# Pooled attention with routed experts: longer warm-up, own PSUM banks for the first pooled v, constants on either side of the first pooled k, and search steps moved in front of the last attention tiles

## The chip, the cores and the metric

The kernel runs on one core of one Trainium2 chip. The time is the device time of one execution in microseconds (us), and less is better. Before the change three runs took 638.83, 641.46 and 642.39 us, so the median is 641.46 us. A profile comes from one execution more, whose own device time was 640.09 us.

## What is computed

Attention over keys and values that are averaged in groups of 8 rows, followed by a layer of 8 experts with a greedy assignment of tokens. The sizes are B = 8, H = 8, S = 576, D = 64, N = 4608 tokens of width 512, E = 8 experts of hidden width 1024, and cap = N / E = 576 tokens for each expert.

```python
# k_p, v_p: mean over 8 rows in sequence (72 rows left)
attn = softmax(q @ k_p.T / 8); x = (attn @ v_p) as (N, 512)
logits = x @ w_gate                      # (N, 8)
# greedy: pairs (token, expert) by falling logit; a pair is taken when the token
# is still free and the expert holds fewer than cap tokens
for e in range(8):
    out[tokens of e] = relu(x[tokens of e] @ w1[e]) @ w2[e]
```

## The kernel before

The program has two parts. There is no scheduler: each engine runs its instructions in the order in which the Python code issues them, so the place of a call in the code is its place in the queue of every engine that it uses.

**Attention** (class `Attention`) works on 36 tiles of 128 rows. A batch has four and a half tiles, so tile 4 is the first that also holds rows of batch 1. For each tile TensorE makes the scores of all heads (`st_s`, L205, into the PSUM tile `pss`, which has one buffer), VectorE takes the maximum and subtracts it (`softmax`, L215 and L216), ScalarE takes the exponential (L217), TensorE transposes the result in two groups (`st_e`, L234, into `pse` and `rt`), ScalarE copies it out (`eT`, L235), TensorE multiplies it with the pooled v (`st_av`, L247, into `psa`, two buffers), and VectorE normalizes (`norm`: L259, L262 and L272, with the gate logits `lg` in L265 once for four tiles). The loop in `run` is a pipeline: turn n issues the scores of tile n, the transposes of tile n-1, the product of tile n-2 and the normalization of tile n-3.

Keys and values are pooled by `pool_k` (L146 to L150, into `kblk`) and `pool_v` (L161 to L163 into `vsum`, then the masked copies L167 or L176 into the blocks `vblk`). Batch 0 is pooled by VectorE ahead of tile 0 and in turn 0, in two pieces each since k and v arrive in two pieces; the other batches are pooled by GpSimd while the loop runs. `prep_v` (L186, L188) transposes `vsum`, and `prep_g` (L195, L196) multiplies it with the gate weights `wblk` and puts the result into eight columns of `vblk`. Both take the single PSUM bank `rt`, which the second group of `st_e` also takes. The constants of the routing are made in `Routing.consts`. `warm(n)` issues n products of a matrix of ones, whose result is never used.

**Routing** (class `Routing`) finds the tokens of one expert after the other by a search with four rounds (`search`): VectorE compares the rank of each token with 32 thresholds (`compare`, L563, into `cmp`), TensorE counts (L568 for the first expert), and the range shrinks (L630 and L635). `best` (L511, L514, L517) makes each token's best expert (`oh`) and its place on the scale (`q16`) from the logits. For the first expert both run in part ahead of the end of attention: `after` is a table from a tile number to functions that are called behind this tile's `norm`, and `begin` is called in pieces by `finish`, which handles the last two tiles. `close` turns the result into the expert's number (`eid`, which starts the load of its weights) and its list of rows (L699), which starts the five gathers on GpSimd (L929); then it counts what is taken (`per` L708, `pc` L711, L714, and the small VectorE operations L716 to L736).

**Experts** (function `experts`): the generator `g` of the routing is advanced by `step` at places that estimated times in the code set (`now`, `ready`, `dve`). Before the first expert the code waits for its rows, calls `step(0)` (L1182), splits the first four pieces of the weights (L937 and L941), asks for the other half of them through a copy named `late`, calls `step(0)` again (L1187), issues 8 warm-up products and transposes the first two groups of tokens (`turn`, L961 into `tp`, L963, L965). Then stage 1 (L985) and stage 2 (L1012, L1023) of each expert follow.

Of the kernel before, what the change touches and what calls it, by code (L numbers as in the profile page):

```python
# [9 lines left out]
F32 = mybir.dt.float32  # L10
# [11 lines left out]
class Attention:  # L22
# [44 lines left out]
    def local(self, loc, full, consts, then):  # L67
# [84 lines left out]
    def pool_v(self, b, eng, c=slice(0, 5), first=False):  # L152
# [17 lines left out]
        for m0, m1 in ((0, 1), (1, 2), (2, 5)):  # L170
            m0 = max(m0, c.start)
            if m0 < m1:
                n = m1 - m0
                o = slice(B[m0], B[m1])
                k = (B[m1] - B[m0]) // n
                eng.tensor_tensor(v[:, o, :64].rearrange("p (c i) d -> p c i d", c=n),  # L176
                                  s[:, m0:m1, None, :].to_broadcast([128, n, k, 64]),
                                  self.mask[:, o, None].rearrange("p (c i) d -> p c i d", c=n)
                                  .to_broadcast([128, n, k, 64]), op=OP.mult)
# [10 lines left out]
    def prep_g(self, b):  # L190

        nc = self.nc
        ps = self.psR.tile([128, 512], F32, name="rt")
# [109 lines left out]
    def run(self, ctx, full, consts, after, end, warm):  # L303
# [27 lines left out]
        self.local(ctx.enter_context(tc.tile_pool(name="loc", bufs=1)), full, consts,  # L331
                   lambda: self.pool_k(0, nc.vector, kh))
# [10 lines left out]
        for n in range(nt):  # L343
# [16 lines left out]
            if n == 0:  # L360
                self.pool_v(0, nc.vector, vh[1])
# [16 lines left out]
class Routing:  # L378
# [20 lines left out]
    def consts(self, jp, ident):  # L399
# [13 lines left out]
        nc.vector.tensor_scalar(self.wts, self.i36[:, :8], -1.0, 8.0, op0=OP.mult, op1=OP.add)  # L413
        self.tri = cst.tile([128, 128], BF, name="tri")
# [3 lines left out]
        self.jp = jp  # L418
# [10 lines left out]
        self.upper = cst.tile([128, 1], F32, name="upper")  # L429
        nc.vector.tensor_scalar(self.upper, self.pcol, 64.0, None, op0=OP.is_ge)  # L430
        self.need = cst.tile([128, 8], F32, name="need")
        nc.vector.memset(self.need, float(self.cap))
        self.code = cst.tile([128, NC], F32, name="code")
        nc.vector.memset(self.code, 0.0)
        self.bad = cst.tile([128, 1], F32, name="bad")
        nc.vector.memset(self.bad, 0.0)
        self.gs = [cst.tile([128, 16], BF, name=f"g{i}") for i in range(2)]
        self.shares = cst.tile([128, self.rounds], F32, name="shares")
        for i in range(self.rounds):
            nc.vector.memset(self.shares[:, i:i + 1], (J * SHRINK) ** -i / J)  # L440
# [110 lines left out]
    def search(self, shadow, spare):  # L551
# [18 lines left out]
        for k in range(rounds):  # L570
# [4 lines left out]
            elif k == 0:  # L575

                compare(0, nb - 1)
                yield 0
# [165 lines left out]
    def begin(self, g):  # L744

        next(g)
        self.best(self.NC - 4, self.NC - 2)
# [15 lines left out]
    def phase(self, k):  # L763
# [18 lines left out]
        if k == 0:  # L782
            self.nc.gpsimd.tensor_copy(self.lg0, self.lg)
# [248 lines left out]

@with_exitstack
def kernel(ctx, tc, q, k, v, wblk, moe_w1, moe_w2, out):
# [15 lines left out]
    with ExitStack() as c2:  # L1050
# [3 lines left out]
        A.run(c2, R.ones, lambda: R.consts(A.jp, A.ident), {NC - 11: [step], NC - 10: [step], NC - 9: [step], NC - 5: [lambda: R.best(0, NC - 4)]},  # L1054
# [8 lines left out]
def experts(ctx, tc, g, R, xd, w1, w2, out, ident, cap):  # L1063
# [118 lines left out]
    step(0)  # L1182
# [4 lines left out]
    step(0)  # L1187
# [6 lines left out]
    now, ready, dve = 0.0, 0.0, 2.0  # L1194
# [128 lines left out]
```

## Time and profile before

| | us | where it stands |
|---|---|---|
| device time, median of 3 runs | 641.46 | 638.83 to 642.39 |
| profiled execution, device time | 640.09 | 1.37 below the median |
| its span, first to last instruction | 638.2 | 1.89 less than its device time |
| first scores of tile 0 | 7.66 | rows of TensorE, L205 |
| scores of tile 35, the last | 136.39 | same |
| rows of the first expert known | 161.31 | end of L699 |
| stage 1 of the first expert starts | 168.61 | TensorE, L985 |
| one expert in the middle | 57.4 | 289.4 to 346.8 |
| busy: TensorE, VectorE, ScalarE, GpSimd | 603.2, 396.9, 244.1, 174.0 | first part of the page |

In the rows of the profile PE is TensorE's products, PEld its loads of weights, DVE VectorE, ACT ScalarE, POOL GpSimd and SP the queue that issues most loads. A row of the timeline gives the start, the duration, the engine, the line, the operation, output and input tile with the shape, the number of operations that were merged, and in brackets the idle time before it with what ended that. A row of the table by stretches gives, for each stretch, the busy time of PE, PEld, DVE, ACT and POOL with the number of operations, then the clock granted to TensorE (1.00 is full), the busy share of the transfer engines and GB/s.

### The profile page before, as it was taken

How to read it: one execution, taken by the hardware profiler on the slowest of the kernel's cores; microseconds unless marked ns; L12 is line 12 of the kernel's file. 1: busy time of each engine (PE TensorE's matmuls, PEld its weight loads, DVE VectorE, ACT ScalarE, POOL GpSimd, SP SyncE). 2: the span in 40 equal slices, each digit the busy share in tenths (PEclk: the TensorE clock that was granted, in tenths of full speed). 3: DMA queues.
4: the chain of work that ended last, by engine and by line, in shares of the span. 5: the costliest groups of instructions: out<-in, count | busy, mean ns of one | idle time of the engine just before them, and what ended most of it. 6: DMA issues, size and time to landing. Idle time of an engine off the chain costs nothing.

```text
span 638.2 us, 11819 instructions
## 1 busy us (share of the span) xinstructions
PE 603.2 (95%) x4516; PEld 522.3 (82%) x4516; DVE 396.9 (62%) x1142; ACT 244.1 (38%) x561; POOL 174.0 (27%) x215
## 2 busy tenths in 40 slices
PE   6999999994799999999999999999999999999991
PEld 3899998984598789779977987897799889879980
DVE  7677777888886768766862885386378236506100
ACT  6344444442362335233532433252345225415210
POOL 1999996000300410312111302120230213020011
PEclk9799999997799999999999999999999999999996
DMA  9989982121630743308103701630190054013010
GB/s 359 426 333 385 348 311 84 67 83 51 207 134 1 256 157 123 101 34 298 67 17 113 284 1 49 225 139 18 50 339 8 37 207 170 17 64 128 1 51 29
DMA packets 32578, 92.13 MB, mean 144 GB/s; under 512 B 3456, under 2 KB 3456, under 8 KB 29824
## 3 DMA queue, kind: packets, MB, share of 16 engines
q1 hardware_dynamic: 21296, 62.92, 26.5%
q0 software_dynamic: 5888, 18.88, 8.4%
q10 hardware_dynamic: 5328, 9.48, 3.9%
q8 instruction: 37, 0.61, 0.4%
q14 instruction: 29, 0.24, 0.1%
HBM read 72.40 MB, written 18.87 MB: 143 GB/s over the span
## 4 chain that ended last, share of the span: by engine, by line
PE 72%; issue 14%; DVE 7%; POOL 3%; DMA 2%; ACT 1%; POOLq 0%; SPq 0%; ACTq 0%; DVEq 0%
PE h L985 25%; PE h L1012 20%; PE psa L247 7%; PE pss L205 6%; PE h L1023 3%; PE tp L961 2%; PE pse L234 2%; POOL out_dram L999 1%; PE rt L234 1%; PE rt L195 1%; POOL xg L929 1%; PE rt L688 1%; PE rt L605 1%; PE rt L186 1%; PE rt L568 1%
## 5 line engine op out<-in xcount | busy, mean ns | idle before, releaser
L999 POOL DMA_INDIRECT out_dram<-yt,rows x32 | 33.2, 1036 | 280.5 <-ACT yt L1016 280.1
L1012 PE MATMUL h<-w2l,hh 128*128 128x512 f32 x256 | 102.8, 401 | 0.0
L1012 PE MATMUL h<-w2h,hl 128*128 128x512 f32 x256 | 102.0, 399 | 0.0
L1012 PE MATMUL h<-w2h,hh 128*128 128x512 f32 x256 | 101.2, 395 | 0.0
L985 PE MATMUL h<-xl,w1h 128*128 128x320 f32 (+1 forms) x512 | 95.9, 302 | 0.0
L985 PE MATMUL h<-xh,w1h 128*128 128x320 f32 (+1 forms) x512 | 91.2, 299 | 0.7 <-ACT xh L963 0.7
L985 PE MATMUL h<-xh,w1l 128*128 128x320 f32 (+1 forms) x512 | 91.7, 298 | 0.0
L990 ACT ACTIVATE hh<-h 128x320 fp32r<-128x320 f32 (+1 forms) x128 | 51.9, 409 | 99.1 <-PE h L985 96.9
L985 PEld LDWEIGHTS h<-xh,w1h 128*128 128x128 f32 x512 | 75.3, 189 | 3.6 <-issue 2.7
L985 PEld LDWEIGHTS h<-xl,w1h 128*128 128x128 f32 x512 | 77.0, 190 | 0.7
L985 PEld LDWEIGHTS h<-xh,w1l 128*128 128x128 f32 x512 | 76.1, 189 | 0.2
L965 DVE TENSOR_TENSOR xl<-tp,xh 128x512 fp32r<-128x512 f32 (+1 forms) x40 | 25.3, 633 | 78.7 <-ACT xh L963 78.4
L993 DVE SCALAR_TENSOR_TENSOR hl<-h,hh 128x320 fp32r<-128x320 f32 (+1 forms) x128 | 57.4, 451 | 25.3 <-ACT hr L992 16.3
L929 POOL DMA_INDIRECT xg<-xd,rows x40 | 39.7, 992 | 96.6 <-DVE rows L699 62.9
L1016 ACT ACTIVATE yt<-h 128x512 f32<-128x512 f32 x32 | 19.1, 597 | 119.7 <-PE h L1012 103.8
L247 PE MATMUL psa<-vblk,eT 128*128 128x146 f32 (+3 forms) x400 | 61.9, 303 | 0.0
L1012 PEld LDWEIGHTS h<-w2h,hl 128*128 128x128 f32 x256 | 48.1, 188 | 9.0
L1012 PEld LDWEIGHTS h<-w2l,hh 128*128 128x128 f32 x256 | 48.4, 189 | 8.2
L1012 PEld LDWEIGHTS h<-w2h,hh 128*128 128x128 f32 x256 | 48.2, 188 | 8.3
L247 PEld LDWEIGHTS psa<-vblk,eT 128*128 128x128 f32 (+1 forms) x400 | 52.2, 181 | 1.7 <-DVE xt L272 0.3
L205 PE MATMUL pss<-kblk,rawq 128*128 128x144 f32 (+1 forms) x320 | 45.9, 302 | 3.6 <-DVE e L216 2.8
L941 DVE TENSOR_TENSOR w1l<-raw,w1h 128x512 fp32r<-128x512 f32 x64 | 41.2, 686 | 8.1 <-ACT w1h L937 7.9
(194 smaller groups left out, 905.4 us busy)
## 6 DMA issues: line engine op xcount, KB each, us to landing
raw<-in_moe_w_dram SPq DMA_DIRECT2D x64, 512.0 KB, 6.8
xd<-xt ACTq DMA_DIRECT2D x36, 256.0 KB, 4.3
rawv<-in_v_dram SPq DMA_DIRECT2D x7, 1280.0 KB, 11.5
rawk<-in_k_dram SPq DMA_DIRECT2D x7, 1152.0 KB, 8.1
rawq<-in_q_dram SPq DMA_DIRECT2D x7, 1152.0 KB, 13.5
rawk<-in_k_dram SPq DMA_DIRECT2D x2, 576.0 KB, 4.6
rawv<-in_v_dram SPq DMA_DIRECT2D x1, 768.0 KB, 7.2
rawq<-in_q_dram SPq DMA_DIRECT2D x1, 640.0 KB, 8.7
```

The source lines that it names most:

```text
L205: nc.tensor.matmul(ps[cols, j // 2, 144 * (j % 2):144 * (j % 2) + 144], self.q_of(b, j, n, cols.stop - cols.start), self.kblk[b % 4][:, j] ...
L234: nc.tensor.transpose(ps[:127, 128 * m:128 * m + 128], self.e[i][:, o:o + 127], self.ident)
L247: self.nc.tensor.matmul(o[h], self.eT[i][:, c, h], self.vblk[b % 4][:, self.BLOCKS[c]:self.BLOCKS[c + 1]], start=(c == cs[0]), stop=(c == ...
L929: nc.gpsimd.indirect_dma_start(out=self.xg[:n, t, :], out_offset=None, in_=self.xd, in_offset=bass.IndirectOffsetOnAxis(ap=rows[:n, t:t + ...
L941: self.nc.vector.tensor_tensor(l, raw, h.bitcast(F32), op=OP.subtract)
L965: later(1.3, 0.65, lambda: nc.vector.tensor_tensor(xl, ps[:, :, :n], xh, op=OP.subtract))
L985: nc.tensor.matmul(ps[:, :m], a[:, j, fs], b[:, j, o], start=(n == 0), stop=(n == 11))
L990: nc.scalar.activation(hh[:, f, o], ps[:, :m], AF.Relu)
L993: later(0.65, 0.4, lambda f=f, o=o, m=m, ps=ps: nc.vector.scalar_tensor_tensor(hl[:, f, o], ps[:, :m], 0.0, hh[:, f, o].bitcast(F32), op0= ...
L999: st = nc.gpsimd.indirect_dma_start(out=rows, out_offset=bass.IndirectOffsetOnAxis(ap=idx, axis=0), in_=y, in_offset=None)
L1012: nc.tensor.matmul(ps, a[:, f, o], b[:, f], start=(f == 0 and k == 0), stop=(f == 7 and k == 2))
L1023: nc.tensor.matmul(ps[64 * a:64 * a + 64, :256], self.hr[:, f], self.raw2[e][:, f, 256 * a:256 * a + 256], start=(f == 0), stop=(f == 7))
```

## The change

1. `consts` is split. The first half (numbers 0 to 35, `colv`, `j16`, `pcol`, `wts`, `upper`, `need`, `code`, `bad`, `shares`) now stands ahead of `pool_k(0)`, the rest (`more`: `tri`, `untri`, `spread`, `blk`, `gs`) behind it; before, all of it stood behind.
2. Turn 0 issues 16 warm-up products where it issued 8.
3. `prep_v(0)` and `prep_g(0)` take the two banks of a `psa` buffer in place of `rt`, and `prep_v(0)` stands ahead of the transposes of tile 0. The masked copy of the second piece of the first pooled v (`vblk`, L176) goes from VectorE to GpSimd.
4. For batch 1 `prep_v` is one turn later, and `prep_g` stands inside turn `first[1] + 2` = 6, ahead of the product that needs it.
5. `best` for tiles 0 to 27 is called behind tile 28 (before: tiles 0 to 31 behind tile 31); the large comparison of the first search round is cut into three pieces, of which two stand behind tiles 29 and 30 and the third in `begin`.
6. A new function `wake` gathers 32 rows of the second weights by an indirect transfer on GpSimd, behind tile 30 in the code; its result is not used. The copy of the logits `lg0` goes from GpSimd to ScalarE.
7. Before the first expert the two calls of `step(0)` are taken out, and one stands behind the first two `turn`s, with other estimated times.

```diff
@@ local
-        then()
-        consts()
+        consts()
+        then()
+        more()
@@ pool_v
-                eng.tensor_tensor(v[:, o, :64]...
+                (blocks or eng).tensor_tensor(v[:, o, :64]...
@@ prep_v
-        ps = self.psR.tile([128, 512], F32, name="rt")
+        if b:
+            ps = self.psR.tile([128, 512], F32, name="rt")
+        else:
+            self.ps0 = self.ps.tile([128, 2, 512], F32, name="psa", bufs=2)
+            ps = self.ps0[:, 0]
@@ prep_g
-        ps = self.psR.tile([128, 512], F32, name="rt")
+        ps = self.psR.tile([128, 512], F32, name="rt") if b else self.ps0[:, 1]
@@ run
-            plan(first[b], self.prep_v, b)
-            plan(first[b] + 1, self.prep_g, b)
+            plan(first[b] + (b == 1), self.prep_v, b)
+            if b > 1:
+                plan(first[b] + 1, self.prep_g, b)
...
             if n == 0:
-                warm(8)
+                warm(16)
+            if n == 1:
+                self.prep_v(0)
             if n >= 1:
                 self.st_e(n - 1, 0)
+            if n == first[1] + 2:
+                self.prep_g(1)
...
-            if n == 1:
-                self.prep_v(0)
...
-                self.pool_v(0, nc.vector, vh[1])
+                self.pool_v(0, nc.vector, vh[1], blocks=nc.gpsimd)
@@ search
-                compare(0, nb - 1)
-                yield 0
+                for b0, b1 in ((0, 4), (4, 7), (7, nb - 1)):
+                    compare(b0, b1)
+                    yield 0
@@ begin
+        self.best(self.NC - 8, self.NC - 2)
         next(g)
-        self.best(self.NC - 4, self.NC - 2)
@@ phase
-            self.nc.gpsimd.tensor_copy(self.lg0, self.lg)
+            self.nc.scalar.activation(self.lg0, self.lg, AF.Copy)
@@ new
+def wake(nc, R, wk, w2):
+    row = wk.tile([32, 512], F32, name="norow", bufs=1)
+    nc.gpsimd.indirect_dma_start(out=row, out_offset=None, in_=w2.rearrange("e f d -> (e f) d"),
+                                 in_offset=bass.IndirectOffsetOnAxis(ap=R.ti[:32, 0:1], axis=0))
@@ the table behind tiles
-NC - 5: [lambda: R.best(0, NC - 4)]
+NC - 8: [lambda: R.best(0, NC - 8)], NC - 7: [start], NC - 6: [start, lambda: wake(nc, R, rwk, moe_w2)]
@@ experts
-    step(0)
     w1 = pieces[0] = Pieces(0, X.high1, X.low1)
     for i in range(4):
         w1.next(i < 3)
     X.load_1(behind(0), 2, 4)
-    step(0)
     warm(8)
...
-    now, ready, dve = 0.0, 0.0, 2.0
+    step(0)
+    now, ready, dve = 0.0, 2.6, 2.6
```

Three places show what this does to the queues. The first is TensorE in turns 1 and 2: the scores of tile 1 (`pss`), the transposes of the exponentials `e` and of the pooled sums `vsum`, the gate products (`wblk`), and the scores of tile 2. Before:

```order
L205 MATMUL pss<-kblk_128,rawq 128x144 x4
L234 MATMUL pse<-ident,e 127x128 x3
L234 MATMUL rt<-ident,e 127x128 x2
L186 MATMUL rt<-ident,vsum 128x128 x3
L195 MATMUL rt<-wblk,vT 128x40
L195 MATMUL rt<-wblk,vT 128x32
L195 MATMUL rt<-wblk,vT 128x16
L205 MATMUL pss<-kblk_128,rawq 128x144 x4
```

The same stretch of TensorE after the change (line numbers have moved with the code):

```order
L211 MATMUL pss<-kblk_128,rawq 128x144 x4
L192 MATMUL psa<-ident,vsum 128x128 x3
L240 MATMUL pse<-ident,e 127x128 x3
L240 MATMUL rt<-ident,e 127x128 x2
L201 MATMUL psa<-wblk,vT 128x40
L201 MATMUL psa<-wblk,vT 128x32
L201 MATMUL psa<-wblk,vT 128x16
L211 MATMUL pss<-kblk_128,rawq 128x144 x4
```

The transposes of the pooled sums have moved ahead of those of the exponentials, and they and the gate products write to `psa`, so they no longer share a bank with `rt`.

The second is VectorE around the last two tiles: the normalization of tile 31, then the best experts (`bv`, `q16a`, `oh`) and the softmax of tile 35 (`mx`, `e`). Before:

```order
L265 TENSOR_REDUCE lg<-gt_1505 128x32
L272 TENSOR_TENSOR xt<-psa,rinv 128x512
L511 TENSOR_REDUCE bv_241<-lg 128x32
L514 TENSOR_SCALAR q16a<-bv_241,lo_239,scale 128x32
L517 TENSOR_TENSOR oh_243<-lg,bv_241 128x256
L215 TENSOR_REDUCE mx<-pss 128x8
L216 TENSOR_TENSOR e<-pss,mx 128x576
```

After, from the same normalization on, to the third piece of the comparison:

```order
L271 TENSOR_REDUCE lg<-gt_1512 128x32
L278 TENSOR_TENSOR xt<-psa,rinv 128x512
L221 TENSOR_REDUCE mx<-pss 128x8
L222 TENSOR_TENSOR e<-pss,mx 128x576
L265 RECIPROCAL rinv<-psa 128x8
L268 TENSOR_TENSOR gt_1662<-psa,rinv 128x64
L271 TENSOR_REDUCE lg<-gt_1662 128x8
L278 TENSOR_TENSOR xt<-psa,rinv 128x512
```

The three operations of `best` no longer stand between the normalization of tile 31 and the softmax of tile 35; for tiles 0 to 27 they stand four tiles earlier, and tiles 28 to 33 come behind tile 33.

The third is VectorE between the list of rows and stage 1 of the first expert. Before, the counting of what is taken (`per`, `pc`, `left` and on) stands on both sides of the split of the weights (`w1l`) and ahead of the tokens' low parts (`xl`):

```order
L699 CAST rows<-rt 128x5
L703 SCALAR_TENSOR_TENSOR halves<-rt,upper 128x1
L708 TENSOR_TENSOR per<-oh_243,sel 128x288
L711 TENSOR_REDUCE pc<-per 128x8
L941 TENSOR_TENSOR w1l<-raw_1974,w1h 128x512 x4
L1179 COPY late<-eid 1x1
L716 TENSOR_TENSOR left<-need,rt 128x8
```

After the change:

```order
L713 CAST rows<-rt 128x5
L717 SCALAR_TENSOR_TENSOR halves<-rt,upper 128x1
L955 TENSOR_TENSOR w1l<-raw_1985,w1h 128x512 x4
L1202 COPY late<-eid 1x1
L979 TENSOR_TENSOR xl<-tp,xh 128x4x128 x2
L722 TENSOR_TENSOR per<-oh_243,sel 128x288
L725 TENSOR_REDUCE pc<-per 128x8
L1007 SCALAR_TENSOR_TENSOR hl<-h,hh 128x256
L730 TENSOR_TENSOR left<-need,rt 128x8
```

The counting now stands behind the low parts of the first two groups of tokens, inside stage 1 (`hl` is an output of stage 1). On TensorE the product of `pc` (L714) moves with it, from ahead of the 8 warm-up products to behind the third group of tokens.

More of the change, by code (lines that the diff above doesn't have):

```diff
@@ L65, in consts, with local @@
         self.jp = jp
-    def local(self, loc, full, consts, then):
+    def local(self, loc, full, consts, more, then):
         nc = self.nc
@@ L150, in pool_k, with pool_v @@
                 eng.tensor_tensor(self.kblk[b % 4][h, c, y], t2[h, c, 0], t2[h, c, 1], op=OP.add)
-    def pool_v(self, b, eng, c=slice(0, 5), first=False):
+    def pool_v(self, b, eng, c=slice(0, 5), first=False, blocks=None):
         src = self.rv[b]
@@ L301, in finish, with run @@
             self.store(t, xt)
-    def run(self, ctx, full, consts, after, end, warm):
+    def run(self, ctx, full, consts, more, after, end, warm):
         tc, nc = self.tc, self.nc
@@ L417, in consts @@
         nc.vector.tensor_scalar(self.untri, self.tri, -31.0, None, op0=OP.mult)
-        self.jp = jp
         t = cst.tile([128, 32], I32, name="tf")
@@ L1053 @@
         step = lambda: next(bounds, None)
-        A.run(c2, R.ones, lambda: R.consts(A.jp, A.ident), {NC - 11: [step], NC - 10: [step], NC - 9: [step], NC - 5: [lambda: R.best(0, NC - 4)]},
+        start = lambda: next(g)
+        A.run(c2, R.ones, lambda: R.consts(A.jp, A.ident), R.more, {NC - 11: [step], NC - 10: [step], NC - 9: [step], NC - 8: [lambda: R.best(0, NC - 8)],
+                                                       NC - 7: [start], NC - 6: [start, lambda: wake(nc, R, rwk, moe_w2)]},
               R.begin(g), R.warm)
```

29 lines of the change are left out of this document (16 added, 13 removed).

## Prediction

> **What bounds the kernel now.** The page first: the share of TensorE and the line of its granted clock in 40 slices of 16 us.
>
> ```profile
> PE 603.2 (95%) x4516; PEld 522.3 (82%) x4516; DVE 396.9 (62%) x1142; ACT 244.1 (38%) x561; POOL 174.0 (27%) x215
> PEclk9799999997799999999999999999999999999996
> ```
>
> TensorE is the bound except where its clock is low: slice 2 (16 to 32 us) and slices 10 and 11 (144 to 176). A table by stretches then says where it has room.
>
> ```profile
> 14.00:24.00 10.00, 8.83 (x37) 8.17 (x38) 6.63 (x9) 3.11 (x8) 8.52 (x5) 0.52 1.01 428
> 112.00:137.00 25.00, 24.75 (x200) 22.58 (x199) 20.11 (x51) 11.04 (x23) 0.00 (x0) 1.00 0.20 74
> 137.00:146.00 9.00, 7.62 (x77) 6.93 (x76) 8.44 (x29) 4.01 (x14) 0.00 (x0) 1.00 0.24 89
> 158.00:169.00 11.00, 6.81 (x64) 3.80 (x65) 8.58 (x27) 4.40 (x7) 4.99 (x6) 0.59 0.62 176
> 169.00:230.00 61.00, 59.65 (x456) 50.01 (x455) 45.24 (x144) 22.35 (x52) 9.44 (x13) 1.00 0.37 129
> ```
>
> TensorE runs at half clock in 14 to 24; from 112 to 137 it is full and VectorE has 4.9 of 25 us free; in 137 to 146 VectorE is full (8.44 of 9); in the first expert TensorE idles only 1.35 us. So there is something to win before 25 us, in 137 to 169, and little after. Stretches of 1 and 2 us show the clock.
>
> ```profile
> 12.00:13.00 1.00, 0.00 (x0) 0.00 (x0) 0.97 (x3) 0.47 (x2) 0.00 (x0) 1.00 0.99 418
> 13.00:14.00 1.00, 0.00 (x0) 0.00 (x0) 0.96 (x3) 1.00 (x6) 0.00 (x0) 0.72 1.04 434
> 23.00:24.00 1.00, 1.00 (x7) 1.00 (x7) 0.96 (x2) 0.30 (x1) 1.00 (x1) 0.66 0.99 420
> 140.00:142.00 2.00, 0.84 (x5) 0.68 (x6) 1.90 (x7) 0.68 (x1) 0.00 (x0) 1.00 0.00 0
> ```
>
> TensorE stands still in 12 to 14 and the clock falls to half at 13.4 (0.72 is 0.44 us at 1 and the rest at one half); it returns only at 23.7, though TensorE is 88% busy in between. With 0.84 of 2 us busy, in 140 to 142, it holds.
>
> **The first tiles (parts 1 to 4).** The timeline:
>
> ```profile
> 8.78 0.18 DVE L405 CAST i<-ti 128x36 f32<-128x36 int32 x1
> ...
> 9.10 0.22 DVE L415 TENSOR_SCALAR tri<-jp 128x128 bf16<-128x128 int32 x1
> ...
> 9.40 1.89 PE L460 MATMUL rt<-ones 128*128 128x512 bf16 x8
> ...
> 9.88 0.14 DVE L430 TENSOR_SCALAR upper<-pcol 128x1 f32<-128x1 f32 x1
> 10.55 0.96 DVE L161 TENSOR_TENSOR t<-rawv 128x768 f32<-128x768 f32 x1
> 13.19 0.76 DVE L216 TENSOR_TENSOR e<-pss,mx 128x576 f32<-128x576 f32 x1
> 14.10 2.26 PE L205 MATMUL pss<-kblk,rawq 128*128 128x144 f32 x8 [2.81 <-DVE e L216]
> 15.19 2.62 POOL L146 TENSOR_TENSOR tk<-rawk 128x1152 f32<-128x1152 f32 x1 [12.85 <-DMA rawk<-in_k_dram]
> 15.37 2.73 DVE L176 TENSOR_TENSOR vblk<-vsum,mask 128x256 f32<-128x256 f32 x1
> 19.44 1.63 POOL L150 TENSOR_TENSOR kblk<-tk 64x288 f32<-64x288 f32 x2
> ...
> 25.14 1.14 PE L205 MATMUL pss<-kblk,rawq 128*128 128x144 f32 x8
> ...
> 26.68 1.65 POOL L176 TENSOR_TENSOR vblk<-vsum,mask 128x128 f32<-128x128 f32 x3
> ...
> 136.39 1.22 PE L205 MATMUL pss<-kblk,rawq 128*128 128x144 f32 x8
> ```
>
> VectorE runs without a pause from 8.78, the first constant, to 13.95, the end of tile 0's subtraction, and tile 1's scores wait for that since `pss` has one buffer. The constants that move ahead of k (8.78 to 9.10, and from 9.88 some 0.2 us) are about 0.55 us. VectorE idles 0.97 us there before k lands, so they cost nothing ahead; should they not fit, they cost 0.55 and gain nothing. Tile 0's subtraction ends at 13.40. The 16 products, at 0.21 to 0.24 each (8 in 1.89), run from 9.40 to about 13.0, still ahead of it: they cost nothing, and the gap of 2.81 us becomes 0.4.
>
> So tile 1's scores start at about 13.45 and not 14.10, at full clock: 1.14 and not 2.26 us. The pooled sums were complete when the block product started at 15.37, which is 1.42 us after the subtraction; now that is 14.8. The block product takes VectorE 2.73 us for 256 elements, beside GpSimd's L146; on GpSimd three of them with 704 elements (11 blocks of 64) take 1.65, so this one takes 0.6. It stands ahead of GpSimd's first pooled k, which so ends near 21.5 and not 21.07 (19.44 + 1.63); tile 4 asks for that at about 24.
>
> For the next two tiles I take the steady pace: from 25.14 (tile 3) to 136.39 (tile 35) it is 111.25 / 32 = 3.48 us per tile. Tile 3 then starts at 13.45 + 6.95 = 20.4 and not 25.14: **-4.7**. The chain of tile 1 could beat it by half a us (-5.2). At half clock the two tiles would take what they take now, 25.14 - 14.10 = 11.0, which leaves -0.65. I take -4.7, since the gaps left (0.4 ahead of tile 1's scores, 0.25 behind) are far below the 2.81 that lost the clock. The loop behind is 99% TensorE (24.75 of 25), so the lead stays.
>
> Part 4 costs a wait once: the product of tile 4 stands right behind the gate products of batch 1 and their copy on VectorE. The short VectorE operations quoted here take 0.14 to 0.40, and there is a hand-over on either side: between 0 and 0.6 us; I take **+0.3**.
>
> **The end of attention (part 5).** The timeline:
>
> ```profile
> 137.79 0.40 DVE L511 TENSOR_REDUCE bv<-lg 128x32 f32<-128x256 f32 x1
> 138.78 0.75 DVE L215 TENSOR_REDUCE mx<-pss 128x8 f32<-128x576 f32 x1
> 141.16 0.60 PE L234 MATMUL pse<-ident,e 128*127 128x128 f32 x3 [1.38 <-ACT e L217]
> 142.86 0.68 DVE L563 TENSOR_TENSOR cmp<-q16a,j 128x1024 bf16<-128x1024 f16 x1
> 143.46 0.16 DVE L511 TENSOR_REDUCE bv<-lg 128x2 f32<-128x16 f32 x1
> 146.50 0.23 DVE L563 TENSOR_TENSOR cmp<-q16a,j 128x128 bf16<-128x128 f16 x1
> 146.78 0.29 PE L568 MATMUL rt<-oh,cmp 128*32 128x8 bf16 x4 [0.67 <-DVE cmp L563]
> ```
>
> `best` holds tile 35's softmax from 137.79 to 138.78, 0.99 us, and TensorE waits 1.38 for the exponential. Without it everything up to the gates of tile 34 is 0.95 earlier. The comparison goes from 0.60 (142.86 to 143.46) to 0.23 for its last piece, but `best` now covers six columns there and not two, about +0.15. VectorE gains 1.2; TensorE, whose products of tile 35 then end close to the gates, gives back 0.1: **-1.1**. What moves ahead (0.95 behind tile 28, then 0.4 and 0.3) fits into VectorE's free 20%, 0.7 us per tile, with one softmax up to 0.6 late, which the next tile makes up. If it doesn't, 0.6 comes back; ends -0.5 and -1.4.
>
> **Up to the first expert (parts 6 and 7).** The timeline:
>
> ```profile
> 161.14 0.17 DVE L699 CAST rows<-rt 128x5 int32<-128x5 f32 x1 [0.45 <-PE rt L696]
> ...
> 161.77 0.66 DVE L711 TENSOR_REDUCE pc<-per 128x8 bf16<-128x288 bf16 x1
> 162.27 1.17 POOL L929 DMA_INDIRECT xg<-xd,rows  x1 [15.82 <-DMA raw<-in_moe_w_dram]
> ...
> 167.40 0.17 DVE L736 TENSOR_SCALAR pen<-pick 128x8 f32<-128x8 f32 x1
> ...
> 168.61 0.74 PE L985 MATMUL h<-xh,w1h 128*128 128x256 f32 x4 [0.69 <-ACT xh L963]
> ...
> 174.76 0.43 PE L961 MATMUL tp<-ident,xg 64*128 64x64 f32 x4 [0.84 <-DVE late L1179]
> ...
> 198.78 0.39 PE L1012 MATMUL h<-w2h,hh 128*128 128x512 f32 x1
> ...
> 211.74 0.17 DVE L699 CAST rows<-rt 128x5 int32<-128x5 f32 x1 [0.88 <-PE rt L696]
> ...
> 212.17 1.01 POOL L929 DMA_INDIRECT xg<-xd,rows  x1 [5.18 <-DVE rows L699]
> ```
>
> The first gather starts 0.96 us after its rows (161.31 to 162.27) and takes 1.17; the second expert's starts after 0.26 and takes 1.01. If the difference belongs to the first indirect transfer of the program, `wake` takes 0.7 + 0.16 off; if it comes from the many waits ahead of this gather, nothing. Stage 1 starts behind gather, transposes and copies (168.61, on `xh`). I take **-0.6**, nearest the second expert's row. `wake` itself runs on an idle GpSimd (0.00 busy in 112 to 137): 0. ScalarE's copy of `lg0`: some 0.4 us while the search uses VectorE and TensorE, 0.
>
> Moving `per` and `pc` frees TensorE's warm-up products from waiting for `pc` (162.43), and nothing waits for the end of those. In stage 1 the counting adds about 3 us to VectorE (1.1 for `per` and `pc`, 1.85 up to `pen`), where 15.8 of 61 are free. What can be late is the low part of group 2, for which TensorE has a wait of 0.84 already (174.76, put down to `late`, which now follows that low part directly). Ends -0.8 and +3.0; I take 0, since the buffers (five `h`) cover 3 us of delay. Expert 1's rows (211.74) move back by 15 products of stage 2; its 96 long products lie between 198.78 and 230, at most 0.33 each, so that is under 5 us, and 18 us lie between those rows and the end of the stretch that closes at 230: 0.
>
> **Sum.** -4.7 + 0.3 - 1.1 - 0.6 + 0 = -6.1 us, against 640.09 of the profiled execution: 634.0. That lies 1.4 below the median of the runs, so I predict 641.46 - 6.1 = **635.4**.
>
> **Rivals.**
> *The clock falls in tiles 1 and 2 all the same.* Behind tile 1's scores TensorE now has transposes in a row. If these don't keep the clock up, it falls near 16.9, 3.1 of work take 6.2, and it returns a us or so late: +3.5, or 638.9. Against it speaks 140 to 142, where a good half of 0.84 us was transposes, with the clock at 1. The Trainium skill (TensorE: Matmul & The Clock Gate, Part 4: PE-mode transpose) says that a transpose "doesn't count as PE-busy the same way"; by that rule the sum would be -2.6, by the trace's rows -6.1; no run here shows transposes alone. Chance of this rival: 0.12.
> *Stage 1 starts at half clock.* The warm-up products, no longer held to the end of `pc` at 162.43, start near 161.1 and end 1.3 us earlier, with a gap until the tokens; a busy share of 88% in 14 to 24 lifted the clock only at its end. Two to five us at half clock cost 1 to 2.5: 637.2. Chance 0.12.
> *Slower: VectorE's 3 us make gaps through the whole of stage 1 and the clock stays down.* Half clock from 168 costs half of its length: the gain of 6.1 is eaten once it lasts 12 us, and if it lasts to 198.8, where stage 2 starts, it costs 15: 650. Against it: all gaps of 169 to 230 together are 1.35. Chance 0.03.
> *The change doesn't do what it says:* loads or GpSimd's pooling bind tile 4 and the lead is lost there: -1.4, 640. The pooled k is ready 2.5 us ahead by the sum. Chance 0.05.
>
> **Chances and range.** The forecast has 0.68 (632 to 637). A measurement here can tell about 0.5%, or 3.2 us, so faster means under 638.25: the forecast, most of the second rival and a third of the first, 0.82; same 0.14, slower 0.04. The range reaches to the first rival: 631.3 to 639.3.
>
> **What would show it.** Right: a clock of 1 from 7 to 140; tile 3's scores near 20.4; L215 of tile 35 directly behind the normalization; 0.3 us from rows to the first gather; stage 1 near 162.3. Wrong: 0.5 anywhere in 13 to 24, TensorE waiting on `kblk` or `rawq` at tile 4, half clock behind the start of stage 1, or expert 0 longer than 61 us.

## Result and profile after

The changed kernel takes 635.85 us (median of 8 runs, 634.12 to 636.36) and the kernel before 640.06 (8 runs, 638.06 to 642.39): ratio 0.9931, 95% interval 0.9909 to 0.9953. A repeat (a_again) gave 635.85 against 639.99: 0.9933 [0.9908, 0.9958]. The change saves 4.2 us, or 0.7%. The forecast was 635.4, a saving of 6.1; the spans of the two profiled executions differ by 4.35 (638.2 and 633.85).

The page of the changed kernel: busy engines, and the granted clock in 40 slices.

```profile
PE 602.4 (95%) x4524; PEld 520.3 (82%) x4524; DVE 394.1 (62%) x1143; ACT 244.6 (39%) x562; POOL 176.2 (28%) x216
PEclk9999999995899999999999999999999999999996
```

Slice 2 (16 to 32 us) was 7 and is 9. The dip at the search is still there (slices 10 and 11). The table by stretches, with columns as before (PE, PEld, VectorE, ScalarE, GpSimd, then the clock):

```profile
13.00:14.00 1.00, 0.62 (x5) 0.65 (x6) 0.96 (x3) 1.00 (x4) 0.00 (x0) 1.00 0.99 419
14.00:24.00 10.00, 9.97 (x85) 9.22 (x85) 6.63 (x13) 4.81 (x11) 9.00 (x6) 1.00 1.01 425
158.00:161.00 3.00, 1.31 (x8) 0.84 (x8) 1.05 (x3) 1.16 (x2) 2.39 (x3) 1.00 0.75 175
161.00:164.00 3.00, 2.92 (x13) 2.92 (x14) 1.73 (x3) 0.03 (x1) 0.09 (x1) 0.51 0.88 266
169.00:230.00 61.00, 60.37 (x463) 50.63 (x462) 45.12 (x143) 24.52 (x57) 10.13 (x14) 1.00 0.38 129
```

In 14 to 24 TensorE is now busy throughout and at full clock (8.83 busy and 0.52 before). New is the third and fourth row: a pause in 158 to 161 and half clock in 161 to 164, where stage 1 of the first expert starts; in the profile of before, the clock had returned at 167.05, ahead of stage 1 at 168.61. The timeline of the changed kernel, at the places that the prediction used:

```profile
9.15 3.62 PE L473 MATMUL rt<-ones 128*128 128x512 bf16 x16
...
13.38 1.22 PE L211 MATMUL pss<-kblk,rawq 128*128 128x144 f32 x8 [0.61 <-DVE e L222]
...
14.64 0.76 DVE L221 TENSOR_REDUCE mx<-pss 128x8 f32<-128x576 f32 x1
14.71 0.62 POOL L177 TENSOR_TENSOR vblk<-vsum,mask 128x256 f32<-128x256 f32 x1 [12.36 <-DVE vsum L164]
...
15.28 2.63 POOL L147 TENSOR_TENSOR tk<-rawk 128x1152 f32<-128x1152 f32 x1
...
19.38 1.19 PE L211 MATMUL pss<-kblk,rawq 128*128 128x144 f32 x8
...
130.32 0.85 PE L211 MATMUL pss<-kblk,rawq 128*128 128x144 f32 x5
...
139.52 0.29 PE L581 MATMUL rt<-oh,cmp 128*32 128x8 bf16 x4 [0.48 <-DVE cmp L576]
...
153.87 0.17 DVE L713 CAST rows<-rt 128x5 int32<-128x5 f32 x1 [0.44 <-PE rt L710]
154.91 0.98 POOL L943 DMA_INDIRECT xg<-xd,rows  x1 [46.84 <-DMA raw<-in_moe_w_dram]
...
161.08 1.22 PE L999 MATMUL h<-xh,w1h 128*128 128x256 f32 x4 [0.69 <-ACT xh L977]
...
168.80 0.43 PE L975 MATMUL tp<-ident,xg 64*128 64x64 f32 x4 [1.28 <-issue]
...
192.27 0.39 PE L1026 MATMUL h<-w2h,hh 128*128 128x512 f32 x1
...
215.69 0.66 PE L975 MATMUL tp<-ident,xg 128*128 128x128 f32 x4 [0.53 <-DMA xg<-xd,rows]
...
620.03 0.97 POOL L1013 DMA_INDIRECT out_dram<-yh,halves  x1 [2.29 <-ACT yh L1042]
```

Read as a ledger against the rows of before, the lead (how much earlier the same place is reached) is 5.76 us at tile 3 (25.14 to 19.38), 6.07 at tile 35, 7.26 at the last count (146.78 to 139.52) and 7.53 at stage 1 (168.61 to 161.08). Then it shrinks: 6.51 at stage 2, 5.76 at the first expert's end, 5.56 at the last scatter (625.59 to 620.03), 4.35 at the end of the span. So two questions were open: which part of the change makes the 6.07 of the first tiles, and where the other 3.2 went again.

### The profile page after: what moved, and what is told of

The parts are those of the page before. It is cut to its first block, busy times and chain, and to the rows that moved or that the text cites. A ratio compares the mean times of both kernels' runs of the same rounds, so it can differ in the third digit from the quotient of the medians.

```text
span 633.9 us, 11835 instructions
## 1 busy us (share of the span) xinstructions
PE 602.4 (95%) x4524; PEld 520.3 (82%) x4524; DVE 394.1 (62%) x1143; ACT 244.6 (39%) x562; POOL 176.2 (28%) x216
## 4 chain that ended last, share of the span: by engine, by line
PE 61%; POOL 16%; issue 15%; DVE 4%; DMA 2%; ACT 0%; POOLq 0%; SPq 0%; ACTq 0%
PE h L999 27%; PE h L1026 20%; PE h L1037 4%; POOL t L162 3%; POOL tk L147 3%; PE psa L253 2%; PE tp L975 2%; POOL kblk L151 2%; POOL t L163 2%; POOL vblk L177 2%; POOL tk L148 2%; POOL out_dram L1013 1%; PE pss L211 1%; POOL xg L943 1%; POOL vsum L164 1%
## 5 line engine op out<-in xcount | busy, mean ns | idle before, releaser
L1026 PE MATMUL h<-w2h,hh 128*128 128x512 f32 x256 | 102.1, 399 | 0.0
L1026 PE MATMUL h<-w2h,hl 128*128 128x512 f32 x256 | 102.0, 398 | 0.0
L1026 PE MATMUL h<-w2l,hh 128*128 128x512 f32 x256 | 101.8, 398 | 0.0
L1026 PEld LDWEIGHTS h<-w2l,hh 128*128 128x128 f32 x256 | 48.3, 189 | 8.7
L1026 PEld LDWEIGHTS h<-w2h,hl 128*128 128x128 f32 x256 | 48.2, 188 | 8.5
L1026 PEld LDWEIGHTS h<-w2h,hh 128*128 128x128 f32 x256 | 48.3, 189 | 8.3
L955 DVE TENSOR_TENSOR w1l<-raw,w1h 128x512 fp32r<-128x512 f32 x64 | 41.4, 685 | 10.2 <-ACT w1h L951 10.2
L964 DVE TENSOR_TENSOR w2l<-raw,w2h 128x512 fp32r<-128x512 f32 x64 | 43.2, 681 | 2.1 <-ACT w2h L961 2.1
```

The source lines that it names most:

```text
L955: self.nc.vector.tensor_tensor(l, raw, h.bitcast(F32), op=OP.subtract)
L964: self.nc.vector.tensor_tensor(self.w2l[:, i], self.raw2[e][:, i], self.w2h[:, i].bitcast(F32), op=OP.subtract)
L1026: nc.tensor.matmul(ps, a[:, f, o], b[:, f], start=(f == 0 and k == 0), stop=(f == 7 and k == 2))
```

## Experiments

All figures but the last two columns are of the one profiled execution of each kernel, in us. The experiments ran in three groups on three chips, each group beside its own runs of the kernel before. The last column is the ratio to those, and it is the safer one to compare between groups than the medians. "Tail" is from the scores of tile 35 to the first expert's rows; "to s1" from these rows to stage 1; "s1" and "s2" are stage 1 and the first part of stage 2 (L1026) of the first expert; "end" is from the issue of the last scatter to the end of the span.

| kernel | tile 3 | tile 35 | tail | to s1 | s1 | s2 | end | runs, median | ratio to before |
|---|---|---|---|---|---|---|---|---|---|
| before | 25.14 | 136.39 | 24.91 | 7.31 | 30.17 | 26.54 | 12.61 | 640.06 | |
| changed | 19.38 | 130.32 | 23.71 | 7.05 | 31.19 | 27.29 | 13.82 | 635.85 | 0.9931 [0.9909, 0.9953] |
| a_again | 19.32 | 130.31 | 23.71 | 7.35 | 31.25 | 27.33 | 13.74 | 635.85 | 0.9933 [0.9908, 0.9958] |
| a_warm8 | 20.53 | 131.47 | 23.72 | 7.76 | 31.71 | 27.32 | 13.31 | 637.19 | 0.9956 [0.9932, 0.998] |
| b_warm16 | 21.36 | 132.73 | 24.89 | 8.20 | 30.96 | 26.60 | 12.14 | 641.21 | 1.0019 [0.9993, 1.0045] |
| b_warm16_again | 22.31 | 133.67 | 24.91 | 7.56 | 30.75 | 26.60 | 13.87 | 639.52 (1 run) | |
| a_blocks_dve | 19.87 | 130.79 | 23.73 | 7.12 | 31.88 | 27.36 | 12.36 | 636.24 | 0.9934 [0.9909, 0.9958] |
| a_first_only | 19.45 | 130.47 | 24.91 | 8.32 | 31.27 | 26.56 | 12.11 | 634.96 | 0.9902 [0.9866, 0.9939] |
| a_count_old | 19.54 | 130.46 | 23.72 | 8.07 | 30.55 | 26.61 | 13.12 | 635.26 | 0.9927 [0.9903, 0.995] |
| a_g1_early | 19.49 | 130.41 | 23.72 | 7.14 | 31.90 | 27.30 | 13.95 | 636.06 | 0.9919 [0.9887, 0.9951] |
| a_xg_early | 19.55 | 130.49 | 23.73 | 7.35 | 31.37 | 27.30 | 13.65 | 636.10 | 0.9923 [0.9897, 0.995] |
| a_warm_turns | 19.37 | 130.37 | 23.71 | 6.97 | 30.34 | 27.30 | 13.66 | 634.54 | 0.9899 [0.9867, 0.9931] |
| a_no_wake | 19.20 | 130.16 | 23.72 | 8.10 | 31.56 | 27.34 | 13.00 | 636.12 | 0.9936 [0.9913, 0.9959] |
| a_best | 19.62 | 130.56 | 23.73 | 7.54 | 30.51 | 27.29 | 13.95 | 635.23 | 0.992 [0.9893, 0.9948] |

**a_warm8: the changed kernel with the old number of warm-up products.**

```diff
-                warm(16)
+                warm(8)
```

> The changed kernel with 8 products instead of 16 in turn 0. Theory A (the 16 products keep TensorE's clock up): TensorE stands still from about 11.1 to 13.4 us, the clock falls to half for some us behind that, tile 3's scores start at 22 to 25 us and not at 19.4, and the time is 3 to 5 us longer, about 640. Rival B (the gain belongs to VectorE's shorter queue alone; a gap of 2.3 us is too short to lose the clock): tile 3 at 19.4, clock 1 throughout, time unchanged near 635.9.

A row of its table by stretches (the clock is the third from the end), and the gap in its timeline:

```profile
14.00:17.00 3.00, 3.00 (x16) 2.99 (x15) 2.08 (x4) 1.14 (x4) 2.31 (x2) 0.50 1.01 428
```

```profile
13.36 1.75 PE L211 MATMUL pss<-kblk,rawq 128*128 128x144 f32 x8 [2.33 <-DVE e L222]
```

The gap of 2.33 us does lose the clock, and with TensorE busy behind it the clock is back at 17.3, after one step of 3.4 us and not after 10.2 as before. Tile 3 is 1.15 later and the runs 1.3 us longer (637.19 against 635.85), though the intervals of the two ratios overlap. Theory A's mechanism holds in this trace, its size of 3 to 5 us does not. Between the two traces the time at half clock went with how full TensorE was behind the gap (3.00 of 3 us busy here, 8.83 of 10 before); the gaps differ too, 2.33 and 2.81, so that this is the likely reason and not a shown one.

**b_warm16: the other way round, the kernel before with 16 products and nothing else.**

```diff
-                warm(8)
+                warm(16)
```

> The kernel before with 16 products instead of 8 in turn 0, and nothing else of the change. Theory A (clock and VectorE's queue are two separate gains): the clock stays at 1, tile 1 starts at 14.1 as before, VectorE's 2.73 us block product still holds the softmax of tile 1, and tile 3 starts at 22 to 23 us and not at 25.1: time 2 to 3 us shorter than before, about 637.5. Rival B (VectorE's queue alone counts): tile 3 stays at 25, 640. Rival C (the clock is all of it): tile 3 near 20, 635.

The first profile has clock 1 up to 146 and tile 3 at 21.36, better than theory A said. But this execution was the fastest of ten; their median shows no gain at all. A second profile:

> The kernel before with 16 products in turn 0, a second look: its profiled execution was the fastest of ten (638.05 against a median of 641.21). Theory A (with VectorE's queue as before, the clock falls in the first tiles of most executions even with 16 products): half clock somewhere between 13 and 30 us, tile 3 at 23 to 26 us. Theory B (VectorE's masked copy takes 2.7 us in some executions and 0.4 in others, depending on whether GpSimd's pooling of k has begun): tile 3 at 22.5 to 24 with clock 1, and the copy at 2 us or more. Theory C (the loss lies behind attention): tile 3 near 21.4 as in the first look, and a longer stretch at half clock between 140 and 175 us.

The timelines of the two executions of this one kernel, the first profile and then the second, around VectorE's masked copy:

```profile
15.35 0.43 DVE L176 TENSOR_TENSOR vblk<-vsum,mask 128x256 f32<-128x256 f32 x1
15.70 0.75 DVE L215 TENSOR_REDUCE mx<-pss 128x8 f32<-128x576 f32 x1
15.85 2.62 POOL L146 TENSOR_TENSOR tk<-rawk 128x1152 f32<-128x1152 f32 x1 [13.51 <-DVE vblk L176]
```

```profile
14.88 2.62 POOL L146 TENSOR_TENSOR tk<-rawk 128x1152 f32<-128x1152 f32 x1 [12.54 <-DVE vsum L163]
14.92 2.86 DVE L176 TENSOR_TENSOR vblk<-vsum,mask 128x256 f32<-128x256 f32 x1
17.70 0.74 DVE L215 TENSOR_REDUCE mx<-pss 128x8 f32<-128x576 f32 x1
...
19.30 1.25 PE L205 MATMUL pss<-kblk,rawq 128*128 128x144 f32 x8 [1.21 <-DVE e L216]
```

Theory B is shown: the same instruction takes 0.43 us when it starts ahead of GpSimd's addition of k, and 2.86 when GpSimd starts 0.04 us earlier. In the first, GpSimd's addition starts only behind the copy. That is also the 2.73 in the profile before, where GpSimd had started at 15.19 and the copy at 15.37; in both traces the long copy ends 0.28 to 0.29 us behind the end of GpSimd's addition. The Trainium skill (SBUF — State Buffer, "Who interferes with whom") says that a VectorE instruction with two inputs in SBUF contends with a GpSimd instruction that reads SBUF, and that "issue order, not op shape, decides who blocks"; these two traces agree. The wait then costs TensorE 1.21 us in front of tile 2. Theory C is not borne out: the half clock behind attention lasts 17.07 us (147.22 to 164.29), as in the profile before. In neither profile did the clock fall before the search, so theory A got no support, and why the median of ten runs (mean granted clock 0.969 to 0.975 where the two profiled ones have 0.975 and 0.979) lies 1.7 to 3.2 us above the two stays open. The 16 products alone, at any rate, gain nothing that the runs can tell (641.21 against 640.62 for the kernel before beside them).

**a_blocks_dve: the masked copy back on VectorE in the changed kernel.**

```diff
-                self.pool_v(0, nc.vector, vh[1], blocks=nc.gpsimd)
+                self.pool_v(0, nc.vector, vh[1])
```

> The changed kernel with the masked copy of the second piece of the first pooled v on VectorE again. Theory A: the copy takes VectorE 2.7 us (GpSimd 0.62), the softmax of tile 1 starts some 2.1 us later, TensorE waits that long for its exponential, and tile 3 starts at 21.5 to 22 us; time 2 us longer, about 638; if the new gap takes the clock too, tile 3 at 23 to 25 and 640. Rival B (the wait is hidden behind the transposes of the pooled sums): tile 3 within 0.5 us of 19.4, time unchanged.

Its copy started at 14.90, 0.38 ahead of GpSimd's addition, and took 0.43. Tile 3 is 0.49 later, the runs agree within the intervals. Rival B's outcome, but not for rival B's reason: with VectorE's shorter queue the copy came first in this execution, so there was no wait to hide. On GpSimd the copy stands ahead of the addition on its own queue, so it cannot meet it.

**a_first_only: parts 1 to 4 alone.** The counting stands where a_count_old has it, and:

```diff
-                for b0, b1 in ((0, 4), (4, 7), (7, nb - 1)):
-                    compare(b0, b1)
-                    yield 0
+                compare(0, nb - 1)
+                yield 0
...
-        self.best(self.NC - 8, self.NC - 2)
         next(g)
+        self.best(self.NC - 4, self.NC - 2)
...
-            self.nc.scalar.activation(self.lg0, self.lg, AF.Copy)
+            self.nc.gpsimd.tensor_copy(self.lg0, self.lg)
...
+NC - 5: [lambda: R.best(0, NC - 4)]     # no start, no wake
```

> Parts 1 to 4 of the change alone (first tiles); best, the first comparison, the first gather, the copy of the logits and the counting are as in the kernel before. Theory A (the first tiles, with a clock that no longer falls there, carry nearly all of it, and the rest carries the 1.1 us of the tail less the 0.6 that the moved counting costs): tile 35 at 130.3 us as in the changed kernel, the last count 0.7 to 1.2 us later than there, time 636.0 to 637.0, and the runs as close together as those of the changed kernel (within 2 to 3 us and not the 8 us of before). Rival B (parts 5 to 7 carry a good part): 638 or more.

Theory A holds in tile 35, in the tail (24.91, as before the change; 23.71 to 23.73 in all kernels with part 5) and against rival B. The runs are even no slower than those of the whole change (634.96 in 4 runs, where 636.0 to 637.0 was expected; the intervals overlap). So the first tiles carry all of the gain that the runs can tell. How it divides among parts 1 to 4 is known only in part: the 8 additional products are worth 1.15 us in the trace of a_warm8, the place of the masked copy 0.49 in that of a_blocks_dve, and no run takes back the split of the constants, or the own PSUM banks with the earlier `prep_v(0)`. In its one profile the last scatter starts at 621.90, 1.4 to 1.9 us later than in the two of the changed kernel (620.48, 620.03), and a short end of 12.11 hides that in the span. Whether parts 5 to 7 together are worth these 1.4 to 1.9 us in most executions, or nothing, stays open.

**a_count_old: the counting ahead of the warm-up products again.**

```diff
+    step(0)
     late = wk.tile([1, 2], I32, name="late", bufs=1)
...
+    step(0)
     warm(8)
...
-    step(0)
-    now, ready, dve = 0.0, 2.6, 2.6
+    now, ready, dve = 0.0, 0.0, 2.0
```

> The changed kernel with the two step(0) calls where they stood before, so that the counting of the first expert's tokens stands ahead of the 8 warm-up products again. Theory A (moving the counting into stage 1 is what made expert 0 longer by 1.8 us): stage 1 to stage 2 of expert 0 takes 30.2 us and not 31.2, stage 2 to stage 3 takes 26.5 and not 27.3, stage 1 starts 0 to 1.2 us later, and the time is 0.5 to 1.5 us shorter. Rival B (the loss is only the 3.4 us of half clock at the start of stage 1, and that comes and goes with the phase of the clock's grid): stage 2 to stage 3 stays at 27.3, the time moves by under 0.5 us.

s1 is 30.55 and not 31.19, and s2 is 26.61 and not 27.29. Over all traces s2 is 26.54 to 26.61 in the five with the counting as before and 27.29 to 27.36 in the nine with it moved: theory A is shown for this part. The rows put it down to a chain: expert 1's search ends later (its rows are known 55.40 us behind the first expert's in the changed kernel, 51.76 here), so its first gathered tokens are late and TensorE waits 0.53 (the row at 215.69; all waits for them in s2 are 0.63 there and 0.22 here), and one more short product of that search (0.18) falls into stage 2. Stage 1 is shorter although it has half clock here too, for 3.41 us (162.44 to 165.85) where the changed kernel has 3.40. The wait ahead of the last group's transposes is nearly gone, as the second of these rows shows; the changed kernel has 1.28 there (168.80), behind a low part on VectorE (`xl`, until 168.69) that the moved counting stands in front of.

```profile
160.24 1.33 PE L975 MATMUL tp<-ident,xg 128*128 128x128 f32 x8 [1.30 <-DMA xg<-xd,rows]
...
168.76 0.46 PE L975 MATMUL tp<-ident,xg 64*128 64x64 f32 x4 [0.16 <-DVE xl L979]
```

On the other side stage 1 starts 8.07 and not 7.05 behind the rows. The warm-up products wait for `pc` again, but that is not what sets this start: they end at 158.94, and TensorE then stands idle for 1.30 until the first gathered tokens have landed (the first row). Why they land later in this execution stays open. Net -0.6 in the runs, within their scatter.

**a_warm_turns: more warm-up products in front of stage 1.**

```diff
-    warm(8)
+    warm(11)
...
     for t in range(2):
         turn(0, t)
+        warm(3)
```

> The changed kernel with 11 warm-up products ahead of the first two groups of tokens and 3 more behind each of them (17 and not 8). Theory A (the clock falls at 161 us because TensorE stands idle between its 8 products, which end at 157.3, and stage 1): the clock is at 1 when stage 1 starts, the start is up to 0.6 us later or the same, stage 1's first 3.4 us run at full speed, time 0.5 to 1.3 us shorter than the changed kernel's. Rival B (more products only delay the transposes and the clock stays as it is): 0 to 1 us longer.

The same stretch by the table, and stage 1's first products:

```profile
161.00:164.00 3.00, 2.96 (x26) 2.94 (x26) 2.18 (x5) 0.45 (x3) 0.11 (x2) 1.00 0.86 234
```

```profile
161.05 0.73 PE L999 MATMUL h<-xh,w1h 128*128 128x256 f32 x4
```

Theory A: the clock is 1 where it was 0.51, four products take 0.73 and not 1.22, stage 1 starts no later, and s1 is 30.34 and not 31.19. That is 0.85 us in the trace; the runs have 634.54 (4) against 635.85, which points the same way but is within the intervals. For the clock itself the traces agree throughout: in all seven with the counting moved and 8 products stage 1 starts at half clock, and in the two with 17 (this one and a_best) at full clock.

**a_g1_early: the gate products of batch 1 one group earlier.**

```diff
+            if n == first[1] + 2:
+                self.prep_g(1)
             if n >= 1:
                 self.st_e(n - 1, 0)
-            if n == first[1] + 2:
-                self.prep_g(1)
```

> The changed kernel with prep_g(1) directly behind the scores of tile 6, one group of transposes earlier. Theory A (in the changed kernel TensorE waits for VectorE's copy of the gate products ahead of the product of tile 4, since both stand back to back): tile 6 to tile 7 takes 3.6 to 3.8 us and not 4.54, tile 35 starts 0.7 to 0.9 us earlier, time near 635.1. Rival B (the wait only moves: the gate products now wait for vT, or a later tile gives it back): tile 35 within 0.2 us of the changed kernel.

Rival B: tile 6 to 7 takes 4.50, tile 35 does not move. The wait was small and only moved: two products of tile 4 start 0.33 us apart around the end of VectorE's copy in the changed kernel (31.29 and 31.62), and here 0.31 us lie ahead of the gate products instead (30.13 to 30.44). From tile 4 to tile 7 it is 11.26 us before and 11.25 after; the old kernel paid for the same products two tiles earlier.

**a_xg_early: the tokens' tile made before the weights are asked for.**

```diff
+    X.xg = wk.tile([128, 5, 512], F32, name="xg", bufs=1)
+    nc.gpsimd.memset(X.xg[:, :, 0:1], 0.0)
     while (0, "rows") not in since:
```

> The changed kernel with the tile xg made, and touched by one memset on GpSimd, ahead of the search's last steps and of the first load of expert weights. Theory A (the first gather waits 0.87 us behind its rows because its new tile takes over memory whose release it meets only with everything issued up to there, the weight load too): the first gather starts 0.25 to 0.35 us after its rows, and stage 1 of the first expert starts 0.3 to 0.6 us earlier. Rival B (the delay is GpSimd's own at the first gather of tokens): it stays at 0.8 to 0.95 us and nothing moves.

The first gather starts 0.80 us behind its rows (0.88 in the changed kernel), not 0.25: theory A has fallen. The weight load that the trace names as the releaser does not hold the gather through its tile; what does stays open.

**a_no_wake and a_best.** The first is the changed kernel without wake; the second adds the products of a_warm_turns to that.

```diff
-  NC - 6: [start, lambda: wake(nc, R, rwk, moe_w2)]
+  NC - 6: [start]
```

> The changed kernel without wake. Theory A (wake shortens the first gather of tokens by 0.2 us and its wait by 0.1, but lengthens the end: in the traces so far the stretch from the issue of the last scatter to the end of the span is 12.1 to 12.6 us in the three kernels without wake and 12.4 to 14.0 in the seven with it): the gather starts 0.97 us behind its rows and takes 1.17, the last stretch is 12.1 to 12.6 us, and the time is 0.3 to 1.0 us shorter than the changed kernel's. Rival B (the last stretch scatters for another reason, the landing of the last scatter): it is anywhere from 12.1 to 14.0, and the time is 0 to 0.4 us longer.

> The changed kernel without wake and with 11 + 3 + 3 warm-up products ahead of stage 1 of the first expert. If both findings hold, stage 1 starts at full clock, the last stretch is 12.1 to 12.6 us, and the time is 1.3 to 2.3 us shorter than the changed kernel's: near 634. If the last stretch does not depend on wake: 0.7 to 1.0 us shorter, near 634.9.

> The changed kernel as it is, on the same chip as the other kernels of this call, for a second profile and for the comparison: 635.5 to 636.2 us, tile 35 within 0.3 us of 130.3, the last stretch behind the last scatter 12.4 to 14.0 us.

The first two gathers of a_no_wake, and behind them those of a_again:

```profile
154.84 1.16 POOL L943 DMA_INDIRECT xg<-xd,rows  x1 [48.05 <-DMA raw<-in_moe_w_dram]
156.30 1.42 POOL L943 DMA_INDIRECT xg<-xd,rows  x1 [0.30 <-issue]
```

```profile
154.90 0.99 POOL L943 DMA_INDIRECT xg<-xd,rows  x1 [46.73 <-DMA raw<-in_moe_w_dram]
156.19 1.08 POOL L943 DMA_INDIRECT xg<-xd,rows  x1 [0.30 <-issue]
```

The gather without wake behaves as theory A said (0.96 behind the rows, 1.16 long), and the second one is longer too. Over all traces the first gather takes 1.16 to 1.18 in the six without wake and 0.98 to 0.99 in the eight with it. The start of stage 1 does not follow: it is 7.31 to 8.32 behind the rows without wake and 6.97 to 8.07 with it. And the end is 13.00 and, in a_best, 13.95, so that half of theory A has fallen; the time, 636.12, is what rival B gave. a_again came out as expected (635.85, tile 35 at 130.31, an end of 13.74). The two profiles of b_warm16, one kernel, have 12.14 and 13.87. So the end varies by 1.7 us between executions of one kernel. The part that varies is a wait of GpSimd ahead of its closing steps, which begin 2.9 to 4.7 us behind the issue of the last scatter; what it waits for was not settled. a_best is no faster than a_warm_turns (635.23 against 634.54): no version was found that beats the changed kernel by more than the runs can tell.

## Why the prediction came out right

The time was right, and in part by luck: the terms were wrong in both directions, and the saving came out at 4.2 us and not 6.1, from a baseline that was 1.4 us too high. Two signs that the prediction had named for being wrong did appear: half clock behind the start of stage 1, and a first expert longer than 61 us (62.82, and 61.05 before).

- **First tiles, -4.7 predicted.** Mechanism right: no half clock before the search, tile 1's scores at 13.38 (13.45 said), the masked copy 0.62 on GpSimd (0.6 said). The size was short: tile 3 at 19.38 and not 20.4. The step that failed is the pace: 3.48 us per tile is the mean of the whole loop, which contains turns of 3.3 to 3.9 us, among them those with the pooled sums and gate products of the next batch and those with a tile of two batches; plain turns inside a batch take 3.03 to 3.14 in both kernels, and the first two took 3.00 each. By tile 35 the term is -6.07.
- **Part 4, +0.3 predicted:** 0.0 (11.26 and 11.25 from tile 4 to 7).
- **Tail, -1.1 predicted:** -1.20, in every trace with part 5. This term was read correctly from `best` in front of the softmax.
- **First gather, -0.6 predicted.** This step failed. Its wait fell from 0.97 to 0.88, not to 0.3, and its duration from 1.17 to 0.98, and rows to stage 1 is 7.05 and 7.35 in two profiles where it was 7.31 before. What ends TensorE's wait ahead of the first transposes is the landing of the tokens (1.15 and 1.21 us idle in the two profiles), and the prediction counted the gather's issue and not this landing; no gain at stage 1 is shown for wake.
- **First expert, 0 predicted:** +1.8 (stage 1 +1.02, stage 2 +0.75). Stage 1's part has two causes. One is the rival "stage 1 starts at half clock", which came true in both profiles of the changed kernel: in one the clock had returned at 157.66 and fell again at 161.07, in a_again it stayed at half from 141.06 to 164.96. Without it stage 1 is 0.85 shorter (a_warm_turns). The other is the counting: at the same half clock the wait ahead of the last group's transposes is 1.28 with it moved and 0.16 with it as before, and stage 1 is 0.64 shorter (a_count_old). This is the place that the prediction named, with 0.84 in the kernel before at full clock, and set at 0. The two overlap, as they come to more than 1.02 together, and how much each adds is not shown. Stage 2's part is the later search for expert 1 (by a_count_old). The rival's own cause, warm-up products that end earlier, is not the only one: a_first_only and b_warm16, where they still wait for `pc`, start stage 1 at half clock too (s1 31.27 and 30.96, the clock returning at 169.2 and 170.6). The prediction looked only at whether VectorE had room in stage 1 and at 18 us of slack behind expert 1's rows; it did not follow those rows to the gather and the transposes that stand in stage 2.
- **The end, not in the sum:** 12.61 in the profile of before, 13.82 in that of the changed kernel, +1.2, which lies within what one kernel varies by (12.14 and 13.87). It is why the spans differ by 4.35 and not 5.56.
- **The baseline.** The forecast was taken from a median of three runs, 641.46; eight runs gave 640.06. The larger baseline and the too large gain cancel. The profiled execution also lies on the low side by its clock: its mean granted clock is 0.970, where the runs of the kernel before beside the experiments have medians of 0.973 to 0.976 and the changed kernel's have 0.975. How often the clock falls in the first tiles of the kernel before is not shown, since this is its only profile.

The rival "the clock falls in tiles 1 and 2 all the same" did not happen: 1.00 in 14 to 24, with eight transposes in a row from 14.44 to 15.67. Whether transposes count for the clock, the rule that the prediction weighed, the runs do not decide: 1.2 us is a third of one 3.4 us step. Of the rivals, "half clock at stage 1" was not an alternative to the forecast but came true beside it. One slip in the list of signs: by the sum of the terms stage 1 would start at 162.5 and not 162.3; it started at 161.08.

## What to carry to other kernels

Where an instruction's duration in one profile is several times that of its like, look what the neighbouring engine does in that moment: here a start order that varies by half a microsecond between executions decided between 0.43 and 2.86 us, and putting both on one queue takes that race away (in the runs here the difference, 636.24 against 635.85, is within the intervals). Filling an idle stretch of TensorE with useless products kept the clock up in the traces, but alone it gained nothing in the runs: 16 products in the otherwise old kernel gave 641.21 against 640.62. A lead won early has to be followed through every later place that was tuned to the old timing. Judge a change of this size by run medians and by the ledger of start times together: either alone would have misled here, one by its end of the span and the other by three runs.

## What the hardware showed that was not expected

- VectorE's masked copy (two inputs in SBUF) was held 2.86 us by a GpSimd addition that started 0.04 us ahead of it, and took 0.43 alone.
- Half clock after a gap: a gap of 2.81 us was followed by 10.2 us at half clock (13.45 to 23.69) in the kernel before, where 1.17 us in 14 to 24 stayed idle; a gap of 2.33 by 3.4 (13.90 to 17.31) in a_warm8, without idle time behind it. Gaps of 1.07 and 1.08 at the same place (b_warm16, two profiles) did not lose the clock. The changes of the clock in each trace lie whole multiples of 3.41 us apart (10.24, 126.29 and 17.07 us in the kernel before).
- The kernel before varies more between executions than the changed one: 31 runs beside the first set of experiments lie between 636.15 and 644.18 with a mean clock of 0.963 to 0.979, and a clock lower by 0.001 goes with 0.33 us more (correlation -0.83); 14 runs of the changed kernel lie between 634.12 and 637.26 with 0.972 to 0.976.
- From the issue of the last scatter the span goes on for 12.1 to 14.0 us in 14 traces; two executions of one kernel have 12.14 and 13.87. From GpSimd's closing steps on it is 9.26 to 9.36 in all of them, so what varies lies ahead of these.
